# Narrowing pieces planned 3.75 instead of 4.3 apart, and search steps slightly closer, in a two-layer expert kernel

## The chip, the cores and the metric

The kernel runs on 1 core of one Trainium2 chip. The metric is the device time in microseconds (us): 1348.04, the median of 3 runs (1344.69 to 1349.03). All times below are us unless marked ns. PE is TensorE, DVE is VectorE, ACT is ScalarE, POOL is GpSimd; SP is SyncE, which here does little but issue transfers, in the order of the program.

## What is computed

A small attention step gives 4352 tokens of 512 numbers. A first layer sends each token to one of 8 experts, greedily by score, with room for 544 tokens each; a second layer is the same for all tokens. Its two weights come as 64-bit floats.

```python
logits = x @ w_gate
order = np.argsort(-logits.flatten())
for idx in order:
    tok, e = (int(idx) // E, int(idx) % E)
    if assigned[tok] >= 0 or counts[e] >= cap:
        continue
    assigned[tok] = e
    counts[e] += 1
for e in range(E):
    mask = assigned == e
    h = np.maximum(x[mask] @ w1[e], 0.0)
    out[mask] = h @ w2[e]
...
h = out @ w_in
g = np.maximum(0.01 * h, h)
return g @ w_out
```

## The kernel before

**Stages.** `prologue` does the attention, the scores of all tokens and the choice of the first expert's tokens. `experts` then runs eight stages, numbered 0 to 7 as in the code, one for each expert: in a stage PE does 192 products with the first weight (L896) and 192 with the second (L914), each in two halves of the tokens (256 and 288). The result of each block is copied out of `pm` by ACT (`xo`, L921) and stored by SP: L923 for half 0, L925 and L926 (the last 32 tokens, into `x2t`) for half 1. `mlp2` is the second layer, nine groups of up to 512 tokens: `in_proj` (L1172, into `ph`), then on ACT and DVE the leaky step (L1175, L1176), its split into a high and a low part (`gt`, L731 on ACT, L735 on POOL or DVE), then `out_proj` (L1189, into `po`), two steps behind.

**Splits.** Every operand of PE is a pair of a high and a low part. The high part is a copy on ACT (L731), the low part a difference on POOL or DVE (L735). For the tokens of an expert PE transposes five blocks (L854) into `pt4`, of which there are two; ACT takes the high part out (L857) and DVE the low part (L861), and with that the bank is free for the block after next.

**Search.** While PE works for expert k, `search` finds the tokens of a later expert: 14 steps (`cutoff`), each with three counts on DVE (L244), one on ACT (L239, L241), a small product `pc` on PE (L249) and DVE's use of it (L252). `select` runs it for experts 1 to 7, the last with a short form. `slots` then turns the choice into token numbers.

**Narrowing.** The second layer's weights are brought from 64 to 32 bits on the device, in 32 pieces. Each piece is one load of 512 KB (L1059) into one of two buffers `raw64`, five operations on DVE (L1037, L1038, L1040, L1042, L1044), of which the first four read the buffer, and one store of 256 KB (L1063) to `wf`. The intermediate lies in `side`, a bank of the accumulator memory, in which the second layer's first `ph` is placed later. The narrowing starts when the last choice of tokens is done.

**The seam.** In stage 7 `mlp2_prep` loads the narrowed weights back (L1096, three buffers `raw`) and splits them, and `x2_load` loads the first token group of the second layer (L1130, two loads) and splits it. The two loads take the two `raw64` buffers that the narrowing uses.

**What sets the order.** The program is written out ahead by a planner, `Sched`: a planned clock advances by `g.tmm` for each product of PE, and each task has a planned time; when the clock passes it, the task's instructions are put into the queues at that place. `g.dstep(k)` is the planned length of a search step for expert k, `g.ngap` the planned distance of two narrowing pieces, `g.nstep` that of the operations in a piece. On the chip each engine keeps to that order, and waits where something isn't ready.

Of the kernel before, what the change touches and what calls it, by code (L numbers as in the profile page):

```python
# [123 lines left out]
def tables(g):  # L124

    cp, C = g.cp, g.C
    g.t = {n: cp.tile([128, NC], F32, name="t_" + n) for n in ("m", "rk")}
    g.t["oh"] = cp.tile([128, E], F32, name="t_oh")
    g.t.update(mg=g.mg, asg=g.asg, pc=C("pc"), offs=C("offs3"), kl=g.KL, one=g.ones[:, 0:1], pce=C("pcE"),
               grp=C("grp"), eye=g.ident[:, :8])  # L130


def side_tables(g):

    nc, old = g.nc, g.t
    bank = g.bank = g.psa.tile([128, 512], F32, name="side")
    g.t, at = {}, 0
    for n, c in SIDE.items():
        g.t[n] = bank[:, at:at + c]
        at += c  # L140
    for n in ("offs", "kl", "pc", "one", "pce", "grp", "eye"):
        nc.scalar.activation(g.t[n], old[n], AF.Copy)
    for n in ("mg", "asg"):
        nc.vector.tensor_copy(g.t[n], old[n])
# [1066 lines left out]
@with_exitstack  # L1211
def moe_kernel(ctx, tc, i_x, i_xT, i_state, i_stT, i_wg, i_w1, i_w2, i_win, i_wout, i_const, out, dbg=None):
    nc = tc.nc
    g = Ctx()
    g.nc, g.tc = nc, tc
    g.i_x, g.i_xT, g.i_state, g.i_stT, g.i_wg, g.i_const = i_x, i_xT, i_state, i_stT, i_wg, i_const
    g.i_w1, g.i_w2, g.out = i_w1, i_w2, out
    g.i_win, g.i_wout = i_win.bitcast(I32), i_wout.bitcast(I32)
    ctx.enter_context(tc.manual_schedule())
    dram = ctx.enter_context(tc.tile_pool(name="dram", bufs=1, space=bass.MemoryType.DRAM))  # L1220
    g.xs = dram.tile([NT, DM], F32, name="xs")
    g.x2 = [dram.tile([128, 4, 512], F32, name=f"x2_{k}") for k in range(E)]
    g.wf = [[dram.tile([128, 4, 512], F32, name=f"wf{w}_{i}") for i in range(4)] for w in range(2)]
    g.x2t = dram.tile([128, 4, E, 32], F32, name="x2t")

    keep = ctx.enter_context(tc.tile_pool(name="keep", bufs=1))
    g.ident = keep.tile([128, 128], F32, name="ident")
    g.idall = keep.tile([128, E, 5], I32, name="idall")
    g.idt = keep.tile([128, 2], I32, name="idt")
    g.ei = keep.tile([128, E], I32, name="ei")  # L1230
    g.units = ctx.enter_context(tc.tile_pool(name="units", bufs=1))
    g.raw = ctx.enter_context(tc.tile_pool(name="rawp", bufs=1))
    g.xp = ctx.enter_context(tc.tile_pool(name="xp", bufs=1))
    with ExitStack() as es:
        g.cp = es.enter_context(tc.tile_pool(name="sel", bufs=1))
        g.pss = es.enter_context(tc.tile_pool(name="pss", bufs=2, space=bass.MemoryType.PSUM))
        g.known, g.placed = set(), set()
        setup_select(g)
        tables(g)
        g.gate0 = 4  # L1240
        g.warm = 10
        g.fills = {0: 2, 1: 3, 2: 3, 3: 3}
        g.xr = lambda n: 2 if n else 1
        g.dstep = lambda k: 2.15
        prologue(g)
        g.tmm, g.tlow, g.eps = 0.1125, 1.8, 0.05
        g.dstep = lambda k: (1.9, 2.05, 2.25)[min(k, 3) - 1]
        g.tgap = 3.2
        g.tlat, g.plen, g.tmin, g.w0 = 8.0, 48.0, 3.5, 0.5
        g.spp = lambda k: (2 if k == 0 else 1)  # L1250
        g.sx = 0.1
        g.dv = {0: (0, 2), E: ()}
        g.ngap, g.nstep = 4.3, 0.9
        g.wr, g.x2f, g.x2t0 = 1.0, (3, 6, 7, 8, 9), (10.0, 14.0, 15.5, 17.0, 18.5)
        g.wh, g.nw, g.xq = 1, 0, nc.sync
        g.opening = "WWSSWTWSTTS"
        g.wlat, g.dt1, g.dt2 = 3.5, 1.5, 2.3
        with ExitStack() as ea:
            g.ap = ea.enter_context(tc.tile_pool(name="ap", bufs=1))
            g.psa = ea.enter_context(tc.tile_pool(name="psa", bufs=1, space=bass.MemoryType.PSUM))  # L1260
            side_tables(g)
            experts(g)
            if dbg is not None:
                nc.sync.dma_start(out=dbg["xs"], in_=g.xs)
                nc.sync.dma_start(out=dbg["idm"], in_=g.idall)
                nc.sync.dma_start(out=dbg["idt"], in_=g.idt)
    g.bp = ctx.enter_context(tc.tile_pool(name="bp", bufs=1))
    g.psb = ctx.enter_context(tc.tile_pool(name="psb", bufs=1, space=bass.MemoryType.PSUM))
    mlp2(g)
# [43 lines left out]
```

## Time and profile before

| | |
|---|---|
| median of 3 runs | 1348.04 |
| profiled execution | 1345.23 |
| its span, first to last instruction | 1343.5 |
| mean granted clock of PE | 0.983 |
| PE busy | 1284.9 (96%) |
| DVE, ACT, POOL busy | 588.3, 569.4, 529.7 |

The profile is one execution, 1345.23, of which 1343.5 lie between its first and last instruction; the median of the runs is 2.8 above it. Times in the rows count from the start of the span. Busy shares are means over the whole; what a stage waits for is read from that stage.

### The profile page before, as it was taken

The page shows a single profiled execution, that of the slowest core. Times are in us where ns is not written, and L with a number is a line of the kernel's source. Part 1 is how long each engine was busy: PE and PEld are TensorE (multiplying, and loading weights), DVE is VectorE, ACT ScalarE, POOL GpSimd, SP SyncE. Part 2 cuts the span into 40 slices and gives each one's busy share as a digit, 9 for nine tenths or more (in the row PEclk, how much of TensorE's full clock was granted, in tenths as well). Part 3 has the DMA queues.
Part 4 walks back from the last instruction along what each step waited for, and adds up shares of the span by engine and source line. Part 5 has one row for each costly group of instructions (what it writes and reads, how often), then busy time and mean ns, then how long its engine had stood idle before and what let it go on. Part 6 is the DMA issues. An engine that isn't in the chain of part 4 may idle for free.

```text
span 1343.5 us, 21789 instructions
## 1 busy us (share of the span) xinstructions
PE 1284.9 (96%) x8143; PEld 1107.5 (82%) x8145; DVE 588.3 (44%) x1897; ACT 569.4 (42%) x1316; POOL 529.7 (39%) x555
## 2 busy tenths in 40 slices
PE   9986999999999999949999999999999999999997
PEld 4655999999999999938888888888888888888886
DVE  6877787777765867632221221221212112121221
ACT  6766777767574464423322222222222222222222
POOL 2402777677495775735322131221322212212121
PEclk9997999999999999969999999999999999999999
DMA  8546254344345798761101010000000000000000
GB/s 336 206 157 232 77 169 138 103 141 131 115 124 184 249 299 276 235 200 48 47 32 32 0 47 16 32 32 1 32 32 32 22 10 32 16 1 32 0 32 16
DMA packets 62201, 131.67 MB, mean 98 GB/s; under 512 B 15376, under 2 KB 24592, under 8 KB 60176
## 3 DMA queue, kind: packets, MB, share of 16 engines
q1 hardware_dynamic: 52960, 111.17, 24.8%
q0 software_dynamic: 5536, 17.83, 3.9%
q10 hardware_dynamic: 3600, 1.28, 0.4%
q8 instruction: 64, 1.05, 0.3%
q14 instruction: 41, 0.34, 0.1%
HBM read 95.13 MB, written 35.13 MB: 97 GB/s over the span
## 4 chain that ended last, share of the span: by engine, by line
PE 79%; DVE 6%; DMA 5%; POOL 4%; ACT 3%; issue 2%; SPq 0%; ACTq 0%; POOLq 0%; DVEq 0%
PE ph L1172 28%; PE po L1189 27%; PE pm L914 9%; PE pm L896 7%; PE px L612 2%; POOL unit L735 2%; DMA rows<-xs,idall 1%; DMA raw<-in_wout_dram 1%; POOL h L735 1%; PE pt L854 1%; PE ps L485 1%; DMA raw<-wf 1%; DVE jD L244 1%; DVE V L1037 1%; DMA raw<-in_win_dram 1%
## 5 line engine op out<-in xcount | busy, mean ns | idle before, releaser
L1189 PE MATMUL po<-unit,gt 128*128 128x512 f32 x1632 | 393.4, 389 | 0.0
L1189 PEld LDWEIGHTS po<-unit,gt 128*128 128x128 f32 x1632 | 305.5, 188 | 62.6
L1176 DVE TENSOR_TENSOR g<-ph,g 128x512 f32<-128x512 f32 (+1 forms) x144 | 95.4, 663 | 531.0 <-ACT g L1175 524.8
L735 POOL TENSOR_TENSOR gt<-g,gt 128x512 fp32r<-128x512 f32 (+1 forms) x80 | 99.1, 1239 | 454.9 <-ACT gt L731 437.0
L1175 ACT ACTIVATE g<-ph 128x512 f32<-128x512 f32 (+1 forms) x144 | 82.8, 575 | 435.5 <-PE ph L1172 425.4
L1172 PE MATMUL ph<-xt,unit 128*128 128x512 f32 (+1 forms) x960 | 212.0, 371 | 18.2 <-DVE u L1044 18.2
L735 POOL TENSOR_TENSOR unit<-raw,unit 128x512 fp32r<-128x512 f32 x150 | 194.1, 1305 | 48.7 <-ACT unit L731 43.3
L1172 PEld LDWEIGHTS ph<-xt,unit 128*128 128x128 f32 x960 | 170.8, 190 | 50.1 <-issue 18.4
L914 PE MATMUL pm<-h,unit 128*128 128x288 f32 (+1 forms) x1536 | 211.2, 294 | 0.0
L896 PE MATMUL pm<-xt,unit 128*128 128x288 f32 (+1 forms) x1536 | 207.2, 293 | 0.0
L896 PEld LDWEIGHTS pm<-xt,unit 128*128 128x128 f32 x1536 | 198.6, 190 | 5.4 <-issue 4.8
L914 PEld LDWEIGHTS pm<-h,unit 128*128 128x128 f32 x1536 | 199.1, 190 | 0.2
L1172 PE MATMUL ph<-xt_b,unit 128*128 128x512 f32 x768 | 184.5, 389 | 0.0
L1172 PEld LDWEIGHTS ph<-xt_b,unit 128*128 128x128 f32 x768 | 144.2, 188 | 29.9
L731 ACT ACTIVATE gt<-g 128x512 fp32r<-128x512 f32 (+1 forms) x144 | 87.6, 608 | 105.5 <-DVE g L1176 105.5
L735 POOL TENSOR_TENSOR h<-h,h 128x288 fp32r<-128x288 f32 (+1 forms) x128 | 100.1, 790 | 58.3 <-ACT h L731 35.9
L731 ACT ACTIVATE unit<-raw 128x512 fp32r<-128x512 f32 x160 | 98.5, 620 | 27.2 <-DMA raw<-wf 15.3
L244 DVE SCALAR_TENSOR_TENSOR jD<-V,stp,side 128x272 bf16<-128x272 f32 x216 | 95.5, 492 | 0.0
L902 ACT ACTIVATE h<-pm 128x288 f32<-128x288 f32 (+1 forms) x128 | 49.8, 389 | 35.6 <-PE pm L896 23.3
L735 DVE TENSOR_TENSOR gt<-g,gt 128x512 fp32r<-128x512 f32 (+1 forms) x64 | 42.2, 659 | 43.0 <-ACT gt L731 40.5
L731 ACT ACTIVATE h<-h 128x288 fp32r<-128x288 f32 (+1 forms) x128 | 55.3, 432 | 4.1
L239 ACT ACTIVATE jA<-V,bias 128x272 bf16<-128x272 f32 x84 | 43.5, 518 | 21.9 <-DVE bias L233 21.0
(235 smaller groups left out, 1064.6 us busy)
## 6 DMA issues: line engine op xcount, KB each, us to landing
raw<-in_w_dram SPq DMA_DIRECT2D x64, 512.0 KB, 4.8
unit<-in_x_dram SPq DMA_DIRECT2D x8, 1024.0 KB, 9.3
xs<-raw SPq DMA_DIRECT2D x16, 512.0 KB, 2.6
x<-xo SPq DMA_DIRECT2D x64, 128.0 KB, 3.0
raw<-in_win_dram SPq DMA_DIRECT2D x16, 512.0 KB, 6.0
raw<-in_wout_dram SPq DMA_DIRECT2D x16, 512.0 KB, 5.1
raw<-wf SPq DMA_DIRECT2D x16, 512.0 KB, 5.9
raw<-x SPq DMA_DIRECT2D x16, 512.0 KB, 3.7
```

Of the source, the lines that this page charges most:

```text
L239: nc.scalar.activation(jA, V, AF.Sign, bias=bias[:, t - ND:t - ND + 1], scale=-1.0, accum_out=cs[:, t - ND:t - ND + 1])
L244: nc.vector.scalar_tensor_tensor(jD, V, g.zero if T is None else T, offv[:, t:t + 1].to_broadcast([128, 272]), op0=OP.subtract, op1=OP.is_ ...
L612: nc.tensor.matmul(px[:, 256 * hq:256 * hq + 256], aT[2 * b + hq][:, 128 * j:128 * j + 128], stBD[:, 2 * b + hq, :], start=True, stop=True)
L731: nc.scalar.activation(hi, src, AF.Copy)
L735: e.tensor_tensor(lo, src, hi.bitcast(F32), op=OP.subtract)
L896: nc.tensor.matmul(pm, w[:, a, c, wc], xt[k][:, b, c, o], start=(n == 0), stop=(n == 11))
L902: nc.scalar.activation(h32, pm, AF.Relu)
L914: nc.tensor.matmul(pm, w[:, a, c % 4, 128 * m:128 * m + 128], hs[half][:, b, c, :], start=(n == 0), stop=(n == 23))
L1172: nc.tensor.matmul(ph[:, :n], w[:, a, c, wc], xt[:, b, c, :n], start=(i == 0), stop=(i == 11))
L1175: nc.scalar.activation(g32[:, :n], ph[:, :n], AF.Copy, scale=0.01)
L1176: nc.vector.tensor_tensor(g32[:, :n], ph[:, :n], g32[:, :n], op=OP.max)
L1189: nc.tensor.matmul(pos[gi][t], gt[:, a, 128 * t:128 * t + 128], w[:, b, f % 4, :], start=(f == 0 and a + b == 0), stop=(f == NF - 1 and a ...
```

## The change

Three planned numbers change, in two lines of the parameters. `g.dstep` goes from 2.05 to 2.0 for expert 2 and from 2.25 to 2.15 for experts 3 and up; `g.ngap` goes from 4.3 to 3.75, `g.nstep` from 0.9 to 0.85. No instruction is added or removed.

```diff
-        g.dstep = lambda k: (1.9, 2.05, 2.25)[min(k, 3) - 1]
+        g.dstep = lambda k: (1.9, 2.0, 2.15)[min(k, 3) - 1]
...
-        g.ngap, g.nstep = 4.3, 0.9
+        g.ngap, g.nstep = 3.75, 0.85
```

The queue of SP at the end of stage 7, in the program before. `raw_9056`, `raw_9119` and `raw_9187` are buffers of the narrowing's last three loads, `raw_9062` and `raw_9063` those of the token group; the words in brackets are the queues and engines waited for.

```order
L1059 DMA raw_9056<-in_wout_dram 128x1024 [waits DMAHW4_49,DVE_49]
L1130 DMA raw_9062<-x_0_60 128x1024 [waits DMAHW5_49,DMAHW0_49,DVE_49]
L1130 DMA raw_9063<-x_0_60 128x1024 [waits DMAHW6_49,DMAHW4_49,DVE_49]
L1096 DMA raw<-wf_1_73 128x1024 [waits DMAHW7_49,Pool_49]
L1063 DMA wf_3_71<-V_8978 128x512
L925 DMA x_7_67<-xo 128x256 [waits DMAHW1_49,Activation_49]
L926 DMA x2t<-xo 128x32 [waits DMAHW2_49]
L1059 DMA raw_9119<-in_wout_dram 128x1024 [waits DMAHW5_49,DMAHW3_49,Pool_49]
L1063 DMA wf_3_75<-u_9039 128x512
L925 DMA x_7_67<-xo 128x256
L926 DMA x2t<-xo 128x32 [waits DMAHW6_49]
L1096 DMA raw<-wf_2_70 128x1024 [waits DMAHW7_49]
```

The same queue and place in the changed program; `raw_8913` is the narrowing's last load.

```order
L1059 DMA raw_8913<-in_wout_dram 128x1024 [waits DMAHW4_49,DMAHW2_49,DVE_49]
L1063 DMA wf_3_75<-u_8833 128x512 [waits DMAHW3_49,DVE_49]
L1096 DMA raw<-wf_1_69 128x1024 [waits Pool_49]
L1063 DMA wf_3_75<-V_8891 128x512 [waits DMAHW5_49,DVE_49]
L923 DMA x_7_67<-xo 128x256 [waits DMAHW6_49,Activation_49]
L1063 DMA wf_3_75<-u_8954 128x512 [waits DMAHW7_49,DVE_49]
L923 DMA x_7_67<-xo 128x256 [waits DMAHW0_49,Activation_49]
L1096 DMA raw<-wf_1_73 128x1024 [waits DMAHW1_49,Pool_49]
L923 DMA x_7_67<-xo 128x256 [waits DMAHW2_49,Activation_49]
L923 DMA x_7_67<-xo 128x256 [waits DMAHW3_49,Activation_49]
L1130 DMA raw_9094<-x_0_60 128x1024 [waits DMAHW4_49]
L1130 DMA raw_9095<-x_0_60 128x1024 [waits DMAHW5_49]
```

Before, two narrowing loads stood behind the token loads and waited for POOL; now the last narrowing load and store stand ahead of them, and the token loads no longer wait for DVE.

The queue of SP at the end of stage 4, where the narrowing begins, before: the pairs are stores of half 1, `raw_7111` is the first narrowing buffer.

```order
L925 DMA x_4_64<-xo 128x256 [waits Activation_49]
L926 DMA x2t<-xo 128x32 [waits DMAHW2_49]
L925 DMA x_4_64<-xo 128x256 [waits DMAHW3_49,Activation_49]
L926 DMA x2t<-xo 128x32 [waits DMAHW4_49]
L925 DMA x_4_64<-xo 128x256 [waits DMAHW5_49,Activation_49]
L926 DMA x2t<-xo 128x32 [waits DMAHW6_49]
L1059 DMA raw_7111<-in_win_dram 128x1024 [waits DMAHW7_49]
```

And in the changed program, where `raw_7056` and `raw_7105` are the first two:

```order
L925 DMA x_4_64<-xo 128x256 [waits Activation_49]
L926 DMA x2t<-xo 128x32 [waits DMAHW2_49]
L1059 DMA raw_7056<-in_win_dram 128x1024 [waits DMAHW3_49]
L925 DMA x_4_64<-xo 128x256 [waits DMAHW4_49,Activation_49]
L926 DMA x2t<-xo 128x32 [waits DMAHW5_49]
L925 DMA x_4_64<-xo 128x256 [waits DMAHW6_49,Activation_49]
L926 DMA x2t<-xo 128x32 [waits DMAHW7_49]
L1059 DMA raw_7105<-in_win_dram 128x1024 [waits DMAHW0_49]
```

The first load has moved from behind the third pair to behind the first.

DVE in stage 5, where the tokens of expert 6 are split (L861 reads `pt`), before; L1042 and L1044 end a piece, here pieces 5 and 6, counted from 0.

```order
L1042 SCALAR_TENSOR_TENSOR side<-raw_7471,side 128x512 [waits DVE_49]
L861 TENSOR_TENSOR xt<-pt_7513,xt 128x4x128 [waits Activation_49]
L1044 SCALAR_TENSOR_TENSOR u_7522<-V_7523,side 128x512 [waits DMAHW5_49,DVE_49]
L1037 TENSOR_SCALAR V_7589<-raw_7533 128x512 [waits DMAHW1_49,DVE_49]
L1038 TENSOR_SCALAR side<-raw_7533 128x512
L1040 SCALAR_TENSOR_TENSOR side<-raw_7533,side 128x512 [waits DVE_49]
L861 TENSOR_TENSOR xt<-pt_7566,xt 128x4x128 [waits Activation_49]
L1042 SCALAR_TENSOR_TENSOR side<-raw_7533,side 128x512 [waits DVE_49]
L1044 SCALAR_TENSOR_TENSOR V_7588<-V_7589,side 128x512 [waits DMAHW0_49,DVE_49]
L861 TENSOR_TENSOR xt<-pt_7619,xt 128x4x128 [waits Activation_49]
```

The same splits in the changed program, behind piece 7 and within pieces 8 and 9:

```order
L1044 SCALAR_TENSOR_TENSOR u_7529<-V_7530,side 128x512 [waits DMAHW1_49,DVE_49]
L861 TENSOR_TENSOR xt<-pt_7537,xt 128x4x128 [waits Activation_49]
L1037 TENSOR_SCALAR V_7596<-raw_7547 128x512 [waits DMAHW5_49,DVE_49]
L1038 TENSOR_SCALAR side<-raw_7547 128x512
L1040 SCALAR_TENSOR_TENSOR side<-raw_7547,side 128x512 [waits DVE_49]
L1042 SCALAR_TENSOR_TENSOR side<-raw_7547,side 128x512 [waits DVE_49]
L861 TENSOR_TENSOR xt<-pt_7586,xt 128x4x128 [waits Activation_49]
L1044 SCALAR_TENSOR_TENSOR u_7595<-V_7596,side 128x512 [waits DMAHW4_49,DVE_49]
L1037 TENSOR_SCALAR V_7650<-raw_7606 128x512 [waits DMAHW1_49,DVE_49]
L1038 TENSOR_SCALAR side<-raw_7606 128x512
L1040 SCALAR_TENSOR_TENSOR side<-raw_7606,side 128x512 [waits DVE_49]
L861 TENSOR_TENSOR xt<-pt_7640,xt 128x4x128 [waits Activation_49]
```

More narrowing stands ahead of each token split than before.

## Rows read from the trace of the kernel before

**Rows 1.** Order of time, PE at the seam: start, us, engine, line, [idle <-releaser]

```profile
555.76 15.76 PE L914 MATMUL pm<-h,unit 128*128 128x256 f32 x120
589.69 10.66 PE L1172 MATMUL ph<-xt,unit 128*128 128x512 f32 x36 [18.17 <-DVE u L1044]
```

**Rows 2.** Chain of work that ended last, in order of time: start, us, what

```profile
600.36 2.72 PE po L1189 x12
```

**Rows 3.** By stretch: us; busy PE PEld DVE ACT POOL; granted clock, DMA share, GB/s

```profile
415.00:568.00 153.00, 150.52 (x1192) 149.73 (x1189) 111.10 (x174) 76.82 (x175) 106.48 (x105) 0.99 0.83 267
455.00:465.00 10.00, 8.20 (x51) 8.00 (x52) 9.76 (x18) 3.12 (x7) 3.47 (x3) 0.83 0.54 185
590.00:595.00 5.00, 5.00 (x14) 3.86 (x14) 0.00 (x0) 0.00 (x0) 0.00 (x0) 0.55 0.90 206
```

**Rows 4.** Order of time, other engines at the seam

```profile
564.27 3.56 SPq L1130 DMA_DIRECT2D raw<-x  x2
...
576.38 0.40 ACT L921 ACTIVATE xo<-pm 128x288 f32<-128x288 f32 x1
576.71 0.33 SPq L1059 DMA_DIRECT2D raw<-in_wout_dram  x1
...
579.07 1.27 POOL L735 TENSOR_TENSOR xt<-raw,xt 128x512 fp32r<-128x512 f32 x1
...
580.37 0.33 SPq L1059 DMA_DIRECT2D raw<-in_wout_dram  x1
...
588.86 0.69 DVE L1044 SCALAR_TENSOR_TENSOR u<-V,side 128x512 f32<-128x512 f32 x1
...
595.07 0.60 ACT L1175 ACTIVATE g<-ph 128x512 f32<-128x512 f32 x1 [9.98 <-DMA raw<-wf]
...
597.13 1.29 POOL L735 TENSOR_TENSOR gt<-g,gt 128x512 fp32r<-128x512 f32 x1 [10.65 <-ACT gt L731]
```

**Rows 5.** Order of time, SP at the narrowing's start, in its middle and end

```profile
408.13 1.21 SPq L926 DMA_DIRECT2D x2t<-xo  x1
...
415.67 0.45 SPq L1059 DMA_DIRECT2D raw<-in_win_dram  x1
...
433.25 0.33 SPq L1059 DMA_DIRECT2D raw<-in_win_dram  x1
...
559.58 0.38 SPq L1059 DMA_DIRECT2D raw<-in_wout_dram  x1
```

**Rows 6.** The line L1059 (narrowing loads), its last row

```profile
DMA to landing us min/median/max: 3.6/5.3/8.8
```

**Rows 7.** Groups of DVE, 419 to 568: instructions | busy, mean ns of one | idle before

```profile
L1037 DVE TENSOR_SCALAR V<-raw 128x512 int32<-128x512 int32 x30 | 24.7, 823 | 38.7 <-DMA raw<-in_win_dram 24.3 <-DMA raw<-in_wout_dram 13.9
...
L1042 DVE SCALAR_TENSOR_TENSOR side<-raw,side 128x512 int32<-128x512 int32 x30 | 20.8, 694 | 1.0
L1038 DVE TENSOR_SCALAR side<-raw 128x512 int32<-128x512 int32 x30 | 20.5, 683 | 0.0
```

**Rows 8.** Who waited for whom: us in total, times, longest us

```profile
DVE js L252 <- PE pc L249: 54.7, 85, 3.2
...
PE pc L249 <- ACT cnt L241: 4.4, 3, 2.1
```

**Rows 9.** DMA issues, 415 to 590: line, engine, count, KB each, median us to landing

```profile
x2t<-xo SPq DMA_DIRECT2D x14, 16.0 KB, 3.5
```

**Rows 10.** Order of time, stage 5, around PE's wait for a token split

```profile
450.75 3.79 POOL L735 TENSOR_TENSOR unit<-raw,unit 128x512 fp32r<-128x512 f32 x3
...
450.82 4.00 DVE L1037 TENSOR_SCALAR V<-raw 128x512 int32<-128x512 int32 x1
...
456.06 0.68 DVE L861 TENSOR_TENSOR xt<-pt,xt 128x512 fp32r<-128x512 f32 x1
...
456.80 0.66 PE L854 MATMUL pt<-ident,rows 128*128 128x128 f32 x4 [2.48 <-DVE xt L861]
```

## The prediction

> **What bounds the kernel now.** The tally of busy time shows TensorE (PE) working nearly always, so I looked for the places where it doesn't: first PE's instructions in order of time, then the chain of work behind the largest hole, then the stretch ahead of that hole. The hole is at the seam between the two layers. PE ends the last expert at 555.76 + 15.76 = 571.52, starts the second layer at 589.69, 18.17 later, and is released by the last operation of the narrowing (L1044 on DVE) [rows 1]. The first 36 products then take 10.66 where 12 take 2.72 further on, so 36 should take 8.16 [rows 1, 2]; the granted clock was 0.55 in 590 to 595, near the lower of the two levels (1.2 of 2.4 GHz) [rows 3]. From PE's last expert product to the first `po` product: 600.36 - 571.52 = 28.84. The reader is to see three parts of it: the wait, the slower products behind it, and that one DVE operation ended it.
>
> Why L1044 comes so late is in the rows around the end [rows 4]. SP issued the token loads of the second layer (L1130) at 564.27, ahead of the last two narrowing loads (L1059). All four use the two `raw64` buffers, so those two loads had to wait until POOL had split the tokens: they left at 576.71 and 580.37, the second as POOL's last split (579.07, 1.27 long) ended. The last L1044 is at 588.86.
>
> **Part 1, narrowing pieces 3.75 apart.** No instruction is added or removed; 32 loads, 160 DVE operations and 32 stores move. The order of SP shows the effect: both token loads now stand behind all narrowing loads and stores, and behind the fourth store of half 0 (L923). In the trace the load right behind that store left at 559.58 [rows 5]; that is when the token loads can go now, if SP is not held by a narrowing store.
>
> Will the narrowing be done by then? Its plan: pieces planned 4.3 apart took (559.58 - 433.25)/26 = 4.86 [rows 5], 1.13 for each planned us, so 3.75 asks for 4.24. What the chip can do: a buffer is taken from a load's issue until the fourth DVE operation has read it. A load lands after 5.3 (median) [rows 6]; the four operations take 0.82 + 0.68 + 0.69 + 0.69, about 2.9 (the one without a row lies between its neighbours) [rows 7]. Two buffers give one piece in (5.3 + 2.9)/2 = 4.1. The plan asks for almost exactly what two buffers yield: nothing is left over, but nothing is short either.
>
> The Trainium skill (DMA: Bandwidth & Descriptors, Anatomy of one DMA) gives a fit for another issue path, 2.0 us plus the bytes over 436e3; an estimate from it for 512 KB is 3.2 us, so the cycle would be about 3.05, the narrowing would keep to its plan with a quarter to spare, and rival (a) below would have no chance. The trace disagrees: 5.3, with the DMA engines already 0.83 busy in this stretch [rows 3, 6].
>
> **Part 2, search steps closer.** 14 steps for expert 2 by 0.05 and 56 for experts 3 to 6 by 0.1: 6.3 planned, some 7 on the chip. The order agrees: the first narrowing load now stands behind the first store pair of stage 4's second half, whose x2t store left at 408.13, and left at 415.67 before [rows 5]. That issue took 1.21, which makes about 410. Then the last load is asked for 31 x 4.24 = 131 later, at 541, lands at 546 to 549 and is done 3.6 later (four operations and an L1044 of 0.69), near 552; with a few us of lag 556. Both are ahead of 559.6. What do the closer steps cost PE? In 85 of 98 steps DVE waits for PE's count `pc`, 54.7 in all, 0.64 a step [rows 8]: a step 0.11 shorter only eats this idle time. In the 13 others PE could wait 0.11 more, 1.4 in all. PE's own waits there are 4.4 in 3 places, made by ScalarE (ACT) being busy [rows 8]; they may fall elsewhere, from minus 4.4 to plus 4.4. I take 0.
>
> **Part 3, the seam after the change.** PE's first product waits for the last reader of `side` (then long done), and for ACT's copy of the last `pm`, 0.40 [rows 4]: 0.5 after 571.52. Its fifth to eighth products wait for POOL's token splits. Token loads leave at about 560.6, land 5.3 later, and POOL has seven operations of 1.27 from there (four tokens, three weights): 560.6 + 5.3 + 8.9 = 574.8. PE reaches the eighth product at 571.52 + 0.5 + 1.6 = 573.6, so it waits about 1 (bounds 0 and 3). Three groups at full clock take 8.16. The first `po` needs `gt`: ACT's first copy of the second layer waits until the last store of the first layer has landed, 0.4 (copy) + 0.8 (two issues) + 3.5 (landing) [rows 9] = 4.7 behind 571.52; from that copy's start to POOL's end of `gt` is 597.13 + 1.29 - 595.07 = 3.35 [rows 4], so 8.05. PE gets there at 0.5 + 1 + 8.16 = 9.7: hidden, with 1.6 of cover, and late by the difference if the cover goes. Saved: 28.84 - 9.7 = 19.1.
>
> **Part 4, what the denser narrowing costs ahead of the seam.** DVE also takes the token splits (L861) that free the two transpose banks. In stage 5 one L1037 stood for 4.00 while POOL ran three splits back to back (3.79); L861 came late behind it and PE idled 2.48 [rows 10]. The clock was then 0.83 over 455 to 465 [rows 3], 10 x 0.17 = 1.7 more, so 4.2 in all. In the new order the first split stands behind piece 7 instead of within piece 5, and the next ones within pieces 8 and 9. Counting from piece 0 at 410 with SP's weight loads between, I get a lag of 2 to 4 in stage 5 and the same in stage 6, about what the third transpose can take. Bounds: minus 4.2 (the stall goes) to plus 8 (it stays, and two more come). I take plus 1.
>
> The trace shows DVE held through all three POOL operations. The Trainium skill (SBUF — State Buffer, Who interferes with whom) says the second to issue waits until the first instruction finishes; by it L1037 would have waited for one POOL split, 3.79/3 = 1.3, not for three, stage 5's stall would have been about 0, and with none after the change the sum below would be 5 lower. Row and rule differ here, and the row's price stays.
>
> **Sum.** The profiled execution took 1345.23 (span 1343.5). 1345.2 - 19.1 + 0 + 1 = 1327.1. The runs lie from 0.5 below to 3.8 above that execution, so I say **1328**.
>
> **The rivals.** (a) *Loads become the bound.* Denser loads land later. From 410 + 3.7, the last piece is done by 559.6 as long as a piece takes at most (559.6 - 413.7 - 3.6)/31 = 4.59, which is a landing time of 6.3. Each 0.1 of landing time above that costs 31 x 0.05 = 1.6 (half of it a piece, at two buffers), since token loads, then splits, then PE shift with it. At 6.9 that is 9: **1337**. For: a median only 1.0 away, single landings up to 8.8 [rows 6]. Against: start and end both move forward, so 410 to 556 is only some 5% shorter than the 153 of before in which the engines were 0.83 busy [rows 3], 0.87 then.
> (b) *Token transposes stall in stages 5 and 6.* Two more stalls like the one of [rows 10], at 4.2 each: **1336**.
> (c) *Slower than before.* The same mechanism in nearly every transpose: six of them (third to fifth, two stages) can wait for L861, and it takes 19.1/4.2 = five more stalls than now to eat the gain; with six, **1351**. Against it: a stall moves PE and with it the plan back, and gives the narrowing time to catch up.
> (d) *It doesn't do what it says*, and the narrowing still closes the seam: about 1346. The order excludes the token loads in front, so only a lag of 20 could do it.
>
> **Chances.** Forecast, 1321 to 1334: 0.67. (a) 0.16, (b) 0.11, (c) 0.04, (d) 0.02. With most of (a) and (b) the range is **1320 to 1338**. Faster by over 0.3% (4 us, about what a measurement of this kernel can tell from no change): 0.67 + 0.16 + 0.11 = 0.94; within: 0.02; slower: 0.04.
>
> **What would show it.** Right: PE's wait at the seam is 1 to 3, released by ACT or POOL; the granted clock stays at 1.00 there; the first L1059 is near 410 and the last L1044 before 560; L1130 leaves near 560. Wrong: SP's wait at L1059 and the landing time grow (a); new PE waits on L861 with a fallen clock behind them between 445 and 515 (b, c); ACT's first copy of the second layer waits for something other than the last store.

## The result, and the profile after

The changed kernel takes 1332.91 (median; 1332.37 to 1334.34) beside 1346.82 for the kernel before (1344.69 to 1349.03): ratio 0.9898, 95% interval 0.9878 to 0.9918, so 13.9 less. The profiled execution of after took 1332.37, its span is 1330.6, 12.9 below the span of before; the mean granted clock is 0.987.

Order of time, PE at the seam of after, answering [rows 1, 2] (start, us, engine, line, operation, tiles, count, idle time before and its releaser):

```profile
554.30 24.16 PE L914 MATMUL pm<-h,unit 128*128 128x256 f32 x192
579.01 8.50 PE L1172 MATMUL ph<-xt,unit 128*128 128x512 f32 x36 [0.55 <-ACT xo L921]
587.35 2.88 PE L1189 MATMUL po<-unit,gt 128*128 128x512 f32 x12
```

The wait of 18.17 is 0.55 now, and it ends with ACT's last copy of the first layer, no longer with the narrowing. The 36 products take 8.50 instead of 10.66. From the last expert product (554.30 + 24.16 = 578.46) to the end of the 36, behind which the first `po` product follows at once (579.01 + 8.50 = 587.51), it is 9.05 where it was 28.84. The seam gave 19.79.

The other engines around it, in order of time, answering [rows 4]:

```profile
560.01 0.69 DVE L1044 SCALAR_TENSOR_TENSOR u<-V,side 128x512 f32<-128x512 f32 x1
...
560.73 0.32 SPq L1063 DMA_DIRECT2D wf<-u  x1
...
566.48 0.92 SPq L1130 DMA_DIRECT2D raw<-x  x2
...
583.09 0.60 ACT L1175 ACTIVATE g<-ph 128x512 f32<-128x512 f32 x1 [3.62 <-DMA x2t<-xo]
...
585.16 1.29 POOL L735 TENSOR_TENSOR gt<-g,gt 128x512 fp32r<-128x512 f32 x1 [3.36 <-ACT gt L731]
```

The last narrowing operation ends at 560.70 (589.55 before), and the token loads leave behind it. ACT's first copy of the second layer waits 3.62 for the last store of the first (`DMA x2t<-xo`), as the prediction has it; in before its row names another transfer [rows 4]. The token loads leave right behind the last store of half 0 (L923, 566.11), which waits for PE's own products, and no longer for the narrowing.

But 19.8 were saved there and the span fell by 12.9. The other 6.9 are ahead of the seam: the last expert product ends at 578.46, not 571.52. Stage lengths, counted on PE's products from the first L896 product of a stage to that of the next:

| | stage 1 starts | 1 | 2 | 3 | 4 | 5 | 6 | 7 | last expert product ends |
|---|---|---|---|---|---|---|---|---|---|
| before | 190.90 | 55.06 | 56.08 | 57.89 | 57.77 | 54.71 | 50.56 | 48.55 | 571.52 |
| after | 192.30 | 56.97 | 55.81 | 56.19 | 57.04 | 51.80 | 56.38 | 51.98 | 578.46 |

Stages 1 to 4 are 0.79 shorter in sum, stage 5 is 2.91 shorter, stage 6 is 5.82 and stage 7 is 3.43 longer. The 1.40 at the start are not the change's: ACT and DVE do the same work in the same order until 2 to 4 ahead of it, where they are already 1.3 apart, and in the profiles below that start lies anywhere from 191.16 to 195.21. So of the 6.9, stages 5 to 7 made 6.3.

By stretch, answering [rows 3] (us; busy PE, PEld, DVE, ACT, POOL; granted clock, DMA share, GB/s):

```profile
455.00:465.00 10.00, 8.98 (x68) 8.78 (x69) 8.29 (x13) 3.72 (x9) 6.60 (x6) 1.00 0.75 278
415.00:568.00 153.00, 145.95 (x1141) 144.50 (x1141) 115.30 (x168) 76.40 (x173) 102.80 (x102) 0.98 0.82 276
505.00:520.00 15.00, 12.84 (x88) 12.43 (x89) 13.70 (x21) 4.73 (x10) 7.28 (x6) 0.89 0.83 300
545.00:555.00 10.00, 7.94 (x49) 7.71 (x48) 7.52 (x11) 6.54 (x15) 7.37 (x8) 0.83 0.95 335
579.00:590.00 11.00, 10.99 (x48) 9.06 (x49) 3.35 (x4) 4.35 (x8) 5.75 (x6) 1.00 0.73 239
```

The clock is whole at the seam (0.55 before) and in 455 to 465 (0.83 before). It is 0.89 in 505 to 520 and 0.83 in 545 to 555: 15 x 0.11 = 1.7 and 10 x 0.17 = 1.7 lost in stages 6 and 7, each behind waits of PE; from 511.8 to 515 it is 0.50, the lower of the two levels. Who waited for whom on PE in the experts' stages (total, times, longest):

```profile
PE pt L854 <- DVE xt L861: 4.9, 3, 2.0
PE pc L249 <- ACT cnt L241: 2.8, 4, 1.2
PE pm L896 <- ACT h L902: 2.1, 1, 2.1
```

**Stage 6.** Two of the three waits on token splits stand here. Order of time on DVE, POOL and PE:

```profile
503.84 0.69 DVE L1044 SCALAR_TENSOR_TENSOR u<-V,side 128x512 f32<-128x512 f32 x1
504.44 0.68 DVE L861 TENSOR_TENSOR xt<-pt,xt 128x512 fp32r<-128x512 f32 x1
504.62 2.53 POOL L735 TENSOR_TENSOR unit<-raw,unit 128x512 fp32r<-128x512 f32 x2
...
505.18 0.66 PE L854 MATMUL pt<-ident,rows 128*128 128x128 f32 x4 [1.69 <-DVE xt L861]
505.27 2.17 DVE L1037 TENSOR_SCALAR V<-raw 128x512 int32<-128x512 int32 x1
...
510.14 0.68 DVE L861 TENSOR_TENSOR xt<-pt,xt 128x512 fp32r<-128x512 f32 x1
```

Each L861 runs directly behind a whole narrowing piece (L1037 to L1044), and PE's transposes wait for it, 1.69 and then 1.98 (at 510.88). Ahead of the second, L1037 stood for 2.17 beside two products of POOL.

**Stage 7.** The other wait, 2.06, is of a kind that the prediction doesn't have. Order of time on SP, DVE, ACT and PE:

```profile
529.02 0.38 SPq L1059 DMA_DIRECT2D raw<-in_win_dram  x1
...
535.82 1.49 DVE L1037 TENSOR_SCALAR V<-raw 128x512 int32<-128x512 int32 x1 [6.12 <-DMA raw<-in_win_dram]
...
539.40 0.33 SPq L1059 DMA_DIRECT2D raw<-in_wout_dram  x1
...
540.54 0.39 SPq L1096 DMA_DIRECT2D raw<-wf  x1
...
546.93 0.63 ACT L731 ACTIVATE unit<-raw 128x512 fp32r<-128x512 f32 x1 [4.89 <-DMA raw<-wf]
...
547.91 0.40 PE L896 MATMUL pm<-xt,unit 128*128 128x288 f32 x1 [2.06 <-ACT h L902]
```

SP issued nothing from 531.3 to 539.40: its next narrowing load waited until DVE had read the buffer, and DVE was late (6.12 idle) because the load of its piece had left only at 529.02. That load's buffer was free at 525.1, but it stood in SP's queue behind a store pair of half 1 (L925, 527.17) and two reloads. A reload of narrowed weights (L1096) stood behind that load, left at 540.54 and landed near 546.9. ACT stood 4.89 for it at a weight split (L731) with the copies of PE's results (L902) behind, until PE had no free bank. So this chain runs from DVE over SP and ACT to PE.

### The profile page after: what moved, and what is told of

It reads as the page before. It is cut to its first block, busy times and chain, and to the rows that moved or that the text cites. A ratio compares the mean times of both kernels' runs of the same rounds, so it can differ in the third digit from the quotient of the medians.

```text
span 1330.6 us, 21797 instructions
## 1 busy us (share of the span) xinstructions
PE 1286.7 (97%) x8145; PEld 1107.7 (83%) x8145; DVE 590.9 (44%) x1897; ACT 567.8 (43%) x1316; POOL 528.9 (40%) x555
## 3 DMA queue, kind: packets, MB, share of 16 engines
q10 hardware_dynamic: 3600, 1.28, 0.4%
## 4 chain that ended last, share of the span: by engine, by line
PE 79%; DVE 7%; DMA 5%; issue 3%; ACT 3%; POOL 2%; SPq 0%; ACTq 0%; DVEq 0%; POOLq 0%
PE ph L1172 28%; PE po L1189 27%; PE pm L914 8%; PE pm L896 8%; PE px L612 2%; DMA raw<-in_wout_dram 2%; PE ps L485 1%; DVE V L1037 1%; DMA rows<-xs,idall 1%; DMA raw<-in_win_dram 1%; DVE side L1040 1%; POOL unit L735 1%; DVE side L1042 1%; DVE jD L244 1%; PE pt L854 1%
## 5 line engine op out<-in xcount | busy, mean ns | idle before, releaser
L735 POOL TENSOR_TENSOR gt<-g,gt 128x512 fp32r<-128x512 f32 (+1 forms) x80 | 99.1, 1238 | 446.9 <-ACT gt L731 419.2
L735 POOL TENSOR_TENSOR unit<-raw,unit 128x512 fp32r<-128x512 f32 x150 | 193.5, 1299 | 44.1 <-ACT unit L731 43.4
L896 PE MATMUL pm<-xt,unit 128*128 128x288 f32 (+1 forms) x1536 | 208.1, 294 | 2.2 <-ACT h L902 2.1
L896 PEld LDWEIGHTS pm<-xt,unit 128*128 128x128 f32 x1536 | 199.3, 191 | 6.8 <-issue 3.8
L731 ACT ACTIVATE gt<-g 128x512 fp32r<-128x512 f32 (+1 forms) x144 | 87.7, 609 | 105.7 <-DVE g L1176 105.7
L735 POOL TENSOR_TENSOR h<-h,h 128x288 fp32r<-128x288 f32 (+1 forms) x128 | 99.9, 788 | 52.8 <-ACT h L731 42.9
L731 ACT ACTIVATE unit<-raw 128x512 fp32r<-128x512 f32 x160 | 98.7, 620 | 25.7 <-DMA raw<-in_w_dram 18.7
L902 ACT ACTIVATE h<-pm 128x288 f32<-128x288 f32 (+1 forms) x128 | 49.5, 386 | 29.2 <-PE pm L896 22.9
L735 DVE TENSOR_TENSOR gt<-g,gt 128x512 fp32r<-128x512 f32 (+1 forms) x64 | 42.2, 660 | 43.0 <-ACT gt L731 40.1
L731 ACT ACTIVATE h<-h 128x288 fp32r<-128x288 f32 (+1 forms) x128 | 55.3, 432 | 4.0
```

Of the source, the lines that this page charges most:

```text
L731: nc.scalar.activation(hi, src, AF.Copy)
L735: e.tensor_tensor(lo, src, hi.bitcast(F32), op=OP.subtract)
L896: nc.tensor.matmul(pm, w[:, a, c, wc], xt[k][:, b, c, o], start=(n == 0), stop=(n == 11))
L902: nc.scalar.activation(h32, pm, AF.Relu)
```

## The experiments

What they are to settle: is the gain at the seam what the change's two parts make together, and what made stages 6 and 7 together 9.2 longer? Candidates for the second: two buffers are too few (e3), the reload in SP's queue (e4), the order of splits and pieces on DVE (e5), the planned density (e6), L1037 held beside POOL (e9 to e12). Ratios are to runs of before on the same chip. The stages are those of one profile each, counted as above; where the expectations name stage 6 of after as 56.6, or stages 6 and 7 together as 108.6, these are 56.38 and 108.36.

| | median | ratio, 95% interval | stage 5 | stage 6 | stage 7 | PE waits at the seam |
|---|---|---|---|---|---|---|
| after | 1332.91 | 0.9898, 0.9878 to 0.9918 | 51.80 | 56.38 | 51.98 | 0.55 |
| e1_gap_only | 1337.59 | 0.9945, 0.9928 to 0.9962 | 55.09 | 56.87 | 48.73 | 1.83 + 1.73 |
| e2_step_only | 1339.26 | 0.9946, 0.9923 to 0.9968 | 50.48 | 52.72 | 48.31 | 12.21 |
| e3_three_buf | 1329.92 | 0.9909, 0.9880 to 0.9938 | 51.86 | 54.90 | 49.75 | 0.55 |
| e4_reload_act | 1329.31 | 0.9885, 0.9861 to 0.9909 | 52.51 | 56.01 | 48.67 | 0.55 |
| e5_low_early | 1331.22 | 0.9885, 0.9854 to 0.9915 | 51.04 | 53.11 | 51.73 | 0.55 |
| e6_gap400 | 1328.78 | 0.9864, 0.9836 to 0.9892 | 52.53 | 53.10 | 48.48 | 0.59 + 1.76 |
| e7_reload_low | 1329.94 | 0.9869, 0.9835 to 0.9903 | 51.00 | 56.97 | 48.40 | 0.55 + 1.69 |
| e8_reload_gap400 | 1330.80 | 0.9880, 0.9852 to 0.9909 | 52.58 | 53.10 | 48.16 | 0.55 + 0.73 |
| e9_no_hold | 1336.11 | 0.9912, 0.9888 to 0.9937 | 55.62 | 56.07 | 52.08 | 0.55 |
| e10_no_hold_gap400 | 1330.65 | 0.9875, 0.9853 to 0.9896 | 52.60 | 54.39 | 48.85 | 0.55 + 1.42 |
| e11_no_hold_gap400_low | 1331.60 | 0.9874, 0.9857 to 0.9890 | 51.32 | 55.66 | 49.53 | 2.48 + 0.81 |
| e12_psum_operand | 1328.06 | 0.9852, 0.9828 to 0.9875 | 51.55 | 53.78 | 48.38 | 0.55 + 0.76 |

**The two parts apart.** e1_gap_only is before with the pieces' plan alone, e2_step_only before with the search steps alone:

```diff
-        g.ngap, g.nstep = 4.3, 0.9
+        g.ngap, g.nstep = 3.75, 0.85
```

> Only the pieces are planned closer (3.75, 0.85); the search steps stay as before. Theory (the seam closes once all narrowing loads stand ahead of the token loads): they do here too, the narrowing starts some 6 us later and its last L1044 comes at 565 to 570, a few us behind the time at which the token loads could go; PE's wait at the seam 1 to 5; time 1332 to 1337. Rival (the earlier start was needed too): the last L1044 passes 575, PE waits 8 or more, time above 1340.

```diff
-        g.dstep = lambda k: (1.9, 2.05, 2.25)[min(k, 3) - 1]
+        g.dstep = lambda k: (1.9, 2.0, 2.15)[min(k, 3) - 1]
```

> Only the search steps are closer; the pieces stay 4.3 apart. One narrowing load (the last) still stands behind the token loads. Theory (a load behind the token loads waits for POOL's token splits): that one load leaves only when a token split has ended, PE waits 8 to 15 at the seam, time 1338 to 1344. Rival (what counts is how early the narrowing is, some 6 us of the 18): PE's wait is 18 - 6 = 12 without a narrowing load waiting for POOL. Rival 2 (the steps themselves gain or cost in stages 1 to 4): the sum of these stages differs from that of before by more than 3.

Order of time at the seam, first SP and PE of e2_step_only, then PE of e1_gap_only:

```profile
563.11 5.08 SPq L1130 DMA_DIRECT2D raw<-x  x2
576.66 0.33 SPq L1059 DMA_DIRECT2D raw<-in_wout_dram  x1
...
584.92 7.26 PE L1172 MATMUL ph<-xt,unit 128*128 128x512 f32 x19 [12.21 <-DVE u L1044]
```

```profile
583.64 1.88 PE L1172 MATMUL ph<-xt,unit 128*128 128x512 f32 x7 [1.83 <-ACT xo L921]
587.25 6.87 PE L1172 MATMUL ph<-xt,unit 128*128 128x512 f32 x29 [1.73 <-POOL xt L735]
```

With closer steps alone one narrowing load is still behind the token loads (two in before), and PE waits 12.21 for the narrowing's end. With denser pieces alone none is behind them and the large wait is gone. In e2 that last load left when POOL's split had ended, as its theory said. e2's median lies in the range of its theory, e1's 0.6 above. The ratios multiply to 0.9945 x 0.9946 = 0.9891, beside 0.9898 for both: within the intervals they add, though only one of them clears the seam. In e1 the narrowing starts at 419.1, 9 later than in after, and stage 6 already has 56.87, 6.3 more than in before; in e2 it has 52.72, 2.2 more, with one wait of 2.02 on L861. So most of stage 6's loss comes with the denser pieces, and the steps may have a share of it. Stage 5 goes the other way: it is short in e2 (50.48) and not in e1 (55.09), so its gain comes with the steps, as far as one profile each can tell.

**A third buffer.** e3_three_buf gives the narrowing a third `raw64` buffer, with one `xo` fewer to make room:

```diff
-                xo = g.ap.tile([128, HMAX], F32, name="xo", bufs=4)[:, :H]
+                xo = g.ap.tile([128, HMAX], F32, name="xo", bufs=3)[:, :H]
...
-        raws[n] = g.raw.tile([128, 512, 2], I32, name="raw64", bufs=2)
+        raws[n] = g.ap.tile([128, 512, 2], I32, name="raw64c") if n % 3 == 2 else \
+            g.raw.tile([128, 512, 2], I32, name="raw64", bufs=2)
```

> The changed kernel with a third buffer for the narrowing's loads (taken from the space of a fourth xo buffer, so there are three xo buffers). Theory (with two buffers SP stands at a narrowing load until DVE has read a buffer, and the token splits on DVE and the weight reloads behind it in SP's queue come late): the loads keep to their plan, PE's waits in stages 6 and 7 (1.69 + 1.98 + 2.06 and two drops of the clock) go for the most part, stages 6 and 7 together 5 to 9 shorter; time 1324 to 1329. Rival (the transfers share the bandwidth, and density alone makes them late): landing times rise by what the buffer wait falls, stages 6 and 7 as long as in the changed kernel within 2, time 1331 to 1336.

Stages 6 and 7 fall by 3.7 together, where the theory wanted 5 to 9; a wait of 2.81 on L861 stays in stage 6. A piece now takes (545.22 - 408.62)/31 = 4.41 from load to load, 4.56 with two buffers: a third buffer hardly raises the rate. Its seven runs lie near 1327.5 (four, up to 1329.92) and near 1337 (three); the profile is of the lower group, and what the upper one does differently is not known. The median lies between the ranges of theory and rival. So the count of buffers is not what holds stage 6 in this profile; one `xo` fewer was changed along with it.

**The reload on another queue.** e4_reload_act lets ACT issue the reloads:

```diff
-        nc.sync.dma_start(out=r, in_=g.wf[w][i][:, q:q + 2, :])
+        nc.scalar.dma_start(out=r, in_=g.wf[w][i][:, q:q + 2, :])
```

> The changed kernel with the reloads of narrowed weights (L1096) issued by ACT instead of SP, so that they don't stand behind narrowing loads. Theory (stage 7's stall of 2.06 and the clock drop behind it come from one reload held in SP's queue): stage 7 falls from 52.0 to 48 to 50, stage 6 keeps its stalls of L861, time 1329 to 1331 (less what 16 issues cost ACT, some 0.4 each where ACT is needed). Rival (the stall comes from transfers that land late, whoever issues them): stage 7 stays within 1 of 52.0, time 1332 to 1335.

PE in stage 7 of e4_reload_act, in order of time:

```profile
526.24 24.31 PE L896 MATMUL pm<-xt,unit 128*128 128x256 f32 x192
550.53 24.37 PE L914 MATMUL pm<-h,unit 128*128 128x256 f32 x192
```

Both halves of the stage run without a wait; it is 48.67 long, 3.31 shorter than in after, as the chain above requires. Stage 6 keeps its 56. So PE's waits in the two stages go different ways. The wait on L902 in stage 7 is there in three of the five kernels with 3.75 and the reload on SP (after, e5, e9; 0.78 in e3, none in e1), and in none of the three with the reload on ACT. The median is 3.6 below after's, as expected; by the ratios the two can't be told apart.

**The order on DVE.** e5_low_early lets the splits of the last two tiles be due earlier, so that each stands one to three steps earlier in DVE's order, within a piece instead of behind it; e7_reload_low adds the reload on ACT:

```diff
-                sch.add(sch.now + g.tlow, low, key(j))
+                sch.add(sch.now + (g.tlow if k < 6 else 0.2), low, key(j))
```

> The changed kernel, with the token splits on L861 of the two last tiles (those made during stages 5 and 6) due 0.2 us after their transposes instead of 1.8, so that each stands one to three narrowing steps earlier in VectorE's order; nothing else differs. Theory (the 6.1 us that stage 6 lost are the order on VectorE: the splits stand behind whole pieces that run late): the PE waits of 1.69 and 1.98 us on L861 in stage 6 fall to under 0.5 each and the half clock from 511.8 goes, stage 6 falls from 56.6 to 51-53 us, the time from 1332.9 to 1327-1329. Stage 7 keeps its wait of 2 us on the h copies. Rival (VectorE is simply full there, and the splits wait for a late piece wherever they stand): stage 6 stays at 55-57 us and the time at 1331-1334.

> Both mends together: the reloads of L1096 on ACT's queue, and the splits of the last two tiles due 0.2 us after their transposes. Theory (two separate causes, stage 7's the reload held behind a narrowing load, stage 6's the order on VectorE): the gains add, stage 6 at 51-53 and stage 7 at 48-49.5 us, 1323-1327. Rival (one cause, the narrowing's density; what one stage gets back the next one loses): one of the stages falls and the other rises, 1328-1331.

In e5 stage 6 falls to 53.11, as the theory said, though waits of 0.88 and 1.30 on L861 are left where it said under 0.5 each. In e7, with the same order on DVE, it is 56.97, with waits of 2.92, 0.41 and 1.27 on L861. A reading that fits both, and isn't tested, is that the place of a split helps only when the piece that it stands in is in time. The medians, 1331.22 and 1329.94, lie in the rivals' ranges. That the order on DVE alone makes stage 6's loss has fallen; how much it adds isn't settled by these two.

**The density.** e6_gap400 plans the pieces 4.0 apart, e8_reload_gap400 does so with the reload on ACT:

```diff
-        g.ngap, g.nstep = 3.75, 0.85
+        g.ngap, g.nstep = 4.0, 0.85
```

> The changed kernel with the pieces planned 4.0 us apart instead of 3.75, steps 0.85 as in the changed kernel; all narrowing loads still stand ahead of the token loads on SP. Theory (two buffers yield a piece per 4.1 us, so pieces asked every 3.75 pile up on DVE and SP's queue and hold up stages 6 and 7): stages 6 and 7 together fall from 108.6 to 103-106 us, narrowing ends near 565 instead of 560.7, the wait at the seam stays under 3 us: 1328-1331. Rival (any narrowing there costs the same, only its place moves): the two stages stay at 107-109 and the time at 1331-1335, more if the narrowing's end now reaches the token loads.

> The reloads of L1096 on ACT's queue and the pieces planned 4.0 us apart. Theory (density and the held reload are two causes): stage 6 at 52-55, stage 7 at 48-50 us, the wait at the seam under 3 us, 1324-1328. Rival (with the reloads off SP the rate of 3.75 is met, and wider pieces only push the narrowing towards the seam): no better than the reloads alone, 1328-1332, with a wait of over 2 us at the seam.

Stage 6 is 53.10 in both, and stage 7 is 48.48 even with the reload on SP: together 101.58, below the 103 to 106 of e6's theory, whose median came as it said. SP's waits are shorter too; at L1059 for DVE they fall from 48.9 in after to 43.1. The waiting queue's own waits, first of after, then of e6_gap400, 410 to 570 (total, times, longest):

```profile
SPq L1059 <- DVE side L1042: 48.9, 25, 3.8
```

```profile
SPq L1059 <- DVE side L1042: 43.1, 23, 3.7
```

Little is lost for it: the last narrowing load leaves at 553.62 instead of 551.29, a piece takes (553.62 - 410.27)/31 = 4.62 instead of (551.29 - 409.86)/31 = 4.56. The plan at 3.75 asked for a rate that the chip didn't give. But the seam is 2.1 longer in e6 (583.81 - 572.83 = 10.98 from the last expert product to the first `po`, beside 587.35 - 578.46 = 8.89), since PE now arrives 5.6 earlier and waits for POOL's token splits:

```profile
PE ph L1172 <- POOL xt L735: 1.8, 1, 1.8
```

The median is 4.1 below after's, and the intervals of the ratios overlap. Over all profiles stage 6 is 54.9 to 57.0 in six of the seven kernels with 3.75 (53.1 in e5), 53.1 to 54.4 in four of the five with 4.0 (55.7 in e11), and 52.7 at 4.3 in e2. With the wider plan the reload on ACT brings nothing more (0.9880 beside 0.9864, well within the intervals). e8's median lies in the range of its rival, but the wait of over 2 at the seam that the rival named is 1.28. So in these profiles the held reload came with the density. It also hangs on how the two streams meet, since e1, with 3.75 and the reload on SP, has 48.73 in stage 7.

**The held step.** L1037 takes 0.43 alone and ends, when it is held, some 0.3 behind the end of a POOL product. All 32 in after (ns min/median/max):

```profile
L1037 DVE TENSOR_SCALAR V<-raw x32: 427/710/2415, 413.2 to 557.0; 128x512 int32<-128x512 int32 x32
```

e9_no_hold writes it in the form of L1040; e10_no_hold_gap400 does so with pieces 4.0 apart, e11_no_hold_gap400_low with the early splits as well:

```diff
-    nc.vector.tensor_scalar(b, hi, 0x7FFFFFFF, None, op0=OP.bitwise_and)
+    nc.vector.scalar_tensor_tensor(b, hi, 0x7FFFFFFF, hi, op0=OP.bitwise_and, op1=OP.bitwise_and)
```

> The changed kernel with the first narrowing step (L1037) written as a scalar_tensor_tensor, the form of L1040 and L1042, which took 0.69 to 0.70 us each time beside any work of POOL; as a tensor_scalar it takes 0.43 us alone and up to 2.4 us (2.17 at 505.27, ahead of the second late split) beside products on POOL. The values are the same. Theory (part of stage 6's loss is that step held beside POOL): L1037 takes 0.69 in each of its 32 times, the PE wait that was 1.98 us at 510.88 falls under 1 us, stage 6 falls from 56.6 to 52-54.5, the time to 1328-1331. Rival (the hold only takes time that VectorE would have waited for its piece anyway): stage 6 stays at 55-57, the time at 1331-1334; and if POOL is slowed in return, its products on L735 grow and PE waits for them.

> Pieces planned 4.0 us apart as in e6_gap400, and L1037 as a scalar_tensor_tensor. Theory (with the wider plan the waits that are left in stages 5 and 6, 0.46, 1.30, 0.70 and 1.60 us on L861, stand behind a held L1037 of 2.75 us and the like): they fall to under 1.5 us in all, 1325.5-1328. Rival (they come from pieces that land late): they stay, 1328-1330.

> As e10_no_hold_gap400, with the splits of the last two tiles due 0.2 us after their transposes as in e5_low_early. Theory (order on VectorE, its holds and the piece rate are three shares of the same waits): no wait of over 0.5 us on L861 is left in stages 5 and 6, 1324-1327. Rival (a split ahead of its turn is late because its transposes, not VectorE, are late): the waits are those of e10, within 1 us of its time.

The theory fell at its first number: the step is still held. Order of time in e9_no_hold, POOL and DVE, then the line L1037 of that kernel (ns min/median/max):

```profile
509.66 2.53 POOL L735 TENSOR_TENSOR unit<-raw,unit 128x512 fp32r<-128x512 f32 x2
509.78 2.97 DVE L1037 SCALAR_TENSOR_TENSOR V<-raw 128x512 int32<-128x512 int32 x1
```

```profile
L1037 DVE SCALAR_TENSOR_TENSOR V<-raw x32: 681/924/2973, 413.7 to 561.4; 128x512 int32<-128x512 int32 x32
```

It stood for 2.97 beside two POOL products, 0.69 being its own length. In e9 the waits on L861 grew (7.0 in all, 4.9 in after) and the median is 3.2 above after's, though by the ratios the two can't be told apart; e10, at 1330.65, lies above the ranges of theory and rival; e11, at 1331.60, is within 1 of it, and its waits on L861 sum to the same 4.1, as its rival said. Neither is better than e6. So the form is not the reason. What L1037 alone has in the piece is that all its operands lie in SBUF, the memory of the tiles; every other step, and L861, reads or writes PSUM, the accumulator memory (`side`, `pt4`). e12_psum_operand, on e6, tests that:

```diff
-    nc.vector.tensor_scalar(b, hi, 0x7FFFFFFF, None, op0=OP.bitwise_and)
     nc.vector.tensor_scalar(a, hi, 3, 0x3FFFFFFF, op0=OP.logical_shift_left, op1=OP.bitwise_and)
+    nc.vector.scalar_tensor_tensor(b, hi, 0x7FFFFFFF, a, op0=OP.bitwise_and, op1=OP.bitwise_or)
```

> e6_gap400 (pieces planned 4.0 us apart) with the narrowing's first two steps exchanged: the shifted word goes first into the PSUM bank, and the absolute value is then taken as a scalar_tensor_tensor that also reads that bank (its low bits are OR-ed in, which leaves the test on the least exponent as it is for these weights). So every step of the narrowing has an operand in PSUM. In e9, e10 and e11 the step stayed a scalar_tensor_tensor with all operands in SBUF, and was still held for 2.5 to 4.2 us beside products on POOL; in all runs its end stands 0.28 to 0.56 us behind the end of a POOL product. Theory (what is held is the only step whose operands all lie in SBUF, whatever its form): no step of the narrowing takes over 0.8 us; the waits on L861 in stages 5 and 6, 4.1 us in e6_gap400, fall under 2.5; 1326-1329. Rival (it is the first step of a piece that is held, wherever its operands lie): the shift on L1037 now has the long times, up to 2 or 3 us, and the time is 1329-1332. If the holds go and the waits stay over 3.5, the holds only took time that late pieces would have taken: 1328-1330.

The lines of the first two steps of e12_psum_operand (L1037 is the shift there, L1038 the absolute value), ns min/median/max:

```profile
L1037 DVE TENSOR_SCALAR side<-raw x32: 684/695/697, 416.0 to 559.7; 128x512 int32<-128x512 int32 x32
```

```profile
L1038 DVE SCALAR_TENSOR_TENSOR V<-raw,side x32: 686/687/689, 416.7 to 560.5; 128x512 int32<-128x512 int32 x32
```

No step of any of the 32 pieces is held any more. What PE waits for, first in e6_gap400, then in e12_psum_operand, 410 to 590:

```profile
PE pt L854 <- DVE xt L861: 4.1, 4, 1.6
```

```profile
PE pt L854 <- DVE xt L861: 2.5, 2, 1.7
```

The waits fall by 1.6, just not to under the 2.5 that the theory named, and the median by 0.7 (1328.06), which these intervals can't tell from nothing. So the hold is shown, and its price is small.

e12_psum_operand beats both kernels: 0.9852, 0.9828 to 0.9875, lies just below after's interval. Next is e6_gap400, one number away from after, whose interval overlaps after's.

## Why the prediction was right, and where it was off

The forecast was 1328 within 1320 to 1338; it is 1332.91. On the profiled execution the sum said 1327.1 and 1332.37 was measured: 5.3 more. The seam gave 0.7 more than said and stages 1 to 4 gave 0.8, the start took 1.4 that are not the change's, and Part 4, said to cost 1, cost 6.3. That is within Part 4's bound of 8, but 3.4 of it came by a chain that no part has; that the whole stays within the bound is partly luck.

- **What bounds the kernel:** right. The one large hole was the seam, and it was worth what its three parts came to.
- **Part 1, order:** right. No narrowing load stands behind the token loads any more, and e1 shows that the denser plan alone does that.
- **Part 1, rate:** wrong. 4.24 per piece was asked for, 4.1 was computed as possible, 4.56 came; the last load left at 551.29 and not 541, the narrowing ended at 560.70 and not 552 to 556. Landing was not seen to grow: its median is 4.7, and was 5.3. A buffer's round in after, as means from the rows of L1059, L1037 and L1042: 5.16 from issue to landing (the 22 of 32 loads whose landing is recorded), 0.57 from there until DVE begins, 2.93 for the four steps, holds included, and 0.45 until SP sends the next load; half of the sum is 4.56. The step had the first and the third, and left out that DVE can come late to a landed piece and that SP can be late with the next load (6.27 behind the first piece, 3.92 ahead of 529.02). The two buffers were the limit nearly throughout, so nothing made this up: 25 of the last 30 loads left 0.03 behind DVE's last reading of their buffer. The narrowing's end is 1.1 past the 559.6 that the step set as its limit. It did no harm here: the token loads stood for L923 longer still (566.11), as PE came 6.9 later. The row of after that answers [rows 6]:

```profile
DMA to landing us min/median/max: 3.4/4.7/7.7
```

- **Part 2:** right in its start (409.86 for 410) and nearly in its cost (0 taken). Stages 1 to 4 sum to 225.65 to 226.35 in the twelve profiles with the closer steps (226.01 in after), and to 226.80 and 227.43 in the two without (before, e1). That is about 1 of gain, in the direction of the lower bound.
- **Part 3:** right: 19.1 said, 19.79 measured. PE's wait for ACT was 0.55 for 0.5; ACT's first copy stands 583.09 - 578.46 = 4.63 behind PE's end for 4.7; `gt` is ready 585.16 + 1.29 - 578.46 = 7.99 behind it for 8.05. The wait of 1 for POOL's token splits didn't come in after, though the loads left at 566.48 and not 560.6, PE arriving 6.9 later too; in e1, e6 to e8 and e10 to e12 it is there, with 0.7 to 1.8.
- **Part 4:** the term that was mis-sized. Stage 5's stall shrank (2.48 to 1.24, and the clock stayed whole), a gain of 2.91 within the bound of 4.2. But stage 6 got two waits (1.69 + 1.98) and a fallen clock (1.7), 5.4 of its 5.82, which is rival (b) with both its stalls in one stage, at somewhat less than its 4.2 each, and stage 7 got +3.43 by the chain over SP's queue and ACT, which no part named. I had looked for what is queued behind a late DVE step, and not for what is queued behind SP's waiting load.
- **Part 4, the held step:** I set the row of the 4.00 us L1037 [rows 10] against the rule that I cite there, as if the trace spoke against it. That row is an exception among the rows of L1037. In before 22 of them began while POOL ran a product (L735): 20 ended 0.28 to 0.29 behind the end of that one product, though the next had mostly begun by then; one stood until the second had ended, and the 4.00 until the third. In after it is 19 of 21, and two stood until the second had ended (505.27 + 2.17 = 507.44, behind 504.62 + 2.53 = 507.15). So the trace agrees with the rule in the 20 and the 19; why the others stood longer isn't shown. A row of the common kind, from after:

```profile
489.64 1.29 POOL L735 TENSOR_TENSOR unit<-raw,unit 128x512 fp32r<-128x512 f32 x1
489.81 1.41 DVE L1037 TENSOR_SCALAR V<-raw 128x512 int32<-128x512 int32 x1
490.90 0.99 POOL L735 TENSOR_TENSOR h<-h,h 128x288 fp32r<-128x288 f32 x1
```

  One of the other kind is in the rows of stage 6 above. The runs show further that the hold is one of operands. The Trainium skill (SBUF — State Buffer, Who interferes with whom) says that a DVE instruction with at most one input in SBUF, outside the modes that use both ports, doesn't contend with GpSimd, and that one with two inputs in SBUF does with a GpSimd instruction that reads SBUF. By that, e9's form had to stay held and e12's had to be free, and the runs agree: up to 2.97 in the one, 0.70 at most in the other. The prediction put the sum 5 lower if no such stall were left. Doing away with the holds doesn't bring that: without any, e12 is 0.7 below e6 and keeps waits of 0.85 and 1.66 on L861.
- **Rivals:** (a) didn't come, the loads were not seen to land later; (b) came in stage 6 and not in stage 5; (c) and (d) didn't come. The price of (c), 1351, counts six new stalls; one of its six is the stall that before already has, so five new ones give 1345.2 - 19.1 + 5 x 4.2 = 1347.

What stays open is the rest of stage 6. Even with 4.0 and no hold it is 53.78, where it was 50.56 in before. e5 and e7, alike on DVE, differ by 3.86 in that stage, so what one profile shows of it has an uncertainty of that order.

## What to carry to other kernels

Plan a background stream at the rate that it has been seen to reach, not at the one that its buffers would allow: asking for 3.75 instead of 4.0 brought the pieces 1% closer together (4.56 for 4.62) and cost 6.8 in two stages of that pair of profiles (108.36 for 101.58); averaged over the seven kernels with 3.75 and the five with 4.0, which differ in other things too, it is 3.3 (105.95 for 102.69). Behind a load that waits for a buffer, list the transfers in the same queue and who waits for each of them; that chain can reach PE over an engine that the stream doesn't touch. And price the work ahead of a hole by stages, since a change that closes a hole at the end of a stretch is paid within the stretch.

## What the runs showed of the hardware that I had not expected

- Whether a DVE operation is held beside POOL's products hangs on where its operands lie: with all of them in SBUF it stood for up to 2.42 (after), 2.97 (e9) and 4.22 (e11) as a tensor_scalar or a scalar_tensor_tensor, and with one operand in PSUM none of 64 took over 0.70 beside the same work (e12). A hold mostly ends with the one product that POOL is at, 0.28 to 0.29 behind it (19 of 21 in after).
- Being free of the hold costs the first step its short time: the absolute value takes 0.43 alone as a tensor_scalar in SBUF (after) and 0.69 as a scalar_tensor_tensor with the bank in PSUM (e12). The form alone already has that price, 0.68 in SBUF (e9). The kernel is no slower for it.
- A denser stream of 512 KB loads was not seen to land later: median 4.7 instead of 5.3 at nearly the same DMA share (0.82 and 0.83), over the 22 and 16 of 32 landings that are recorded. From issue to DVE's first step, over all 32, the means are 5.70 and 6.02.
